# The first 400 steps of a hand-written schedule in another order: hourglass attention and a gated MLP on one core

## The chip, the core and the metric

The kernel runs on one NeuronCore of one Trainium2 chip. The metric is the device time of one execution in microseconds (us), as a median over several runs. A difference is given against the kernel before, which ran on the same chip. The profile is of one execution of its own, recorded by the hardware profiler, and its times are counted from the start of its span.

## What is computed

The inputs are q, k and v with 8 batches, 8 heads, 576 positions and 64 columns per head, and three weight matrices. Attention is computed twice, once on sequences averaged four to one and once on a band of seven positions, and both results are added. The sum, seen as 4608 tokens of 512 columns, goes through a gated MLP.

```python
q_d = q.reshape(B, H, Sd, 4, D).mean(axis=3)        # k_d, v_d likewise, Sd = 144
out_up = np.repeat(sm_attn(q_d, k_d, v_d), 4, axis=2)
mask = np.abs(pos[:, None] - pos[None, :]) < 4
scores = np.where(mask, scale * q @ k.T, -1e9)      # per head
out_local = softmax(scores) @ v
x = (out_up + out_local).transpose(0, 2, 1, 3).reshape(4608, 512)
out = (np.maximum(x @ w_gate, 0) * (x @ w_val)) @ w_out     # 512 -> 1536 -> 512
```

## The kernel before, in words

The work is cut two ways. Attention goes by pairs of heads: 8 batches of 4 pairs make 32 pairs, counted 0 to 31 (the first batch taken is batch 1). The MLP goes by chunks of 512 tokens, of which there are 9. Four pairs finish one batch of 576 tokens, so chunk 0 can start when pairs 0 to 3 are through attention, and from there on the attention of later pairs runs in between the matmuls of the MLP. The stage until both parts run side by side is the fill.

No scheduler decides the order. `SEQ` (L18 to L233) is one long string of 2097 words, and the last loop of the kernel takes them one after another; `emit_front` (its table is `FRONT_STEPS`) turns each into one or a few instructions. Every engine runs its own instructions strictly in the order of the list, and semaphores make an instruction wait for what it needs. A place in the list is thus a place in the queue of the engine that the step belongs to, and a step that waits holds up all that stands behind it on that engine, and nothing on the others but what depends on it.

The words that matter here, with pair `p`, part `i` and PSUM bank as numbers behind them:

- `loadq/p`, `loadk/p` (L454), `loadv/p` (L504): DMAs issued by GpSimd (POOL), which turn fp32 into fp16 on the way into the tiles `qk16_*` and `vw_*`. `wg/i`, `wv/i` (L1076) and `wo/i` (L1082) are quarters of the weights, 384 KB each, on the same queue. Pair 0's q alone is loaded by SyncE (SP) as fp32 into `q32`, and ScalarE (ACT) turns it into fp16 (`cast`, L1498). From pair 9 on, q and k come in halves (`qk/b0/0@0` and so on, L459).
- `ones/r` (L1504): GpSimd fills the second half of the blocks of `vw_4`, `vw_5` or `vw_6` with ones. `edge/i` (L791) are small fills by VectorE (DVE).
- `tr/p/i` (L540 for pairs 0 to 5, L556 for 6 to 8): TensorE (PE) transposes q and k into PSUM, 24 matmuls for a pair; `ev/p/..` (L576, L579) copies the result to SBUF by ACT or DVE. Later pairs are transposed by a DMA (`flip/p`, L520, on SP).
- `s1/p` (L637, L648): the scores; `ex/p`, `ed/p` (L658, L672): exponentials by ACT; `ma/p` (L664): the band's mask by DVE.
- `vd/p` (L618): six matmuls that pool v; `vc/p` (L627) copies them to SBUF.
- `su/p`, `sd/p` (L697, L685): weighted sums of pairs 0 to 3; `ru`, `tu`, `rd`, `td` (L709 to L728): their division; `xp/p` (L902, L904) and `xe/p` (L914): transposing into `xT`. From pair 4 on the steps are `den` (L738, L747), `num` (L759, L768), `ln`, `inv`, `xn` and `xsum`.
- `hg/j/k`, `hv/j/k` (L919): matmuls of chunk 0 with the gate and the value weights, each group of four followed by `relu` (L928, ACT) and `gate` (L931, DVE). `p/1` to `p/7` (L1004) multiply by the output weights, with sums and differences of blocks made by DVE (`wt`, `sum`, `next`).
- `warm/n` (L1089) and `brief/n` (L1099): n matmuls on zeros whose results nobody reads. Twelve wide ones (128x512) stand ahead of the list.
- `const` (L794): SP overwrites the zeros with a table for later pairs. It must wait for the last `warm`. `v4/a/0@1` (L511) is on SP too: two loads of v for pair 12.

GpSimd's DMAs use eight semaphores in turn, so each one waits until the one eight places ahead of it has landed; from the ninth on the queue is paced by landings.

Of the kernel before, what the change touches and what calls it, by code (L numbers as in the profile page):

```python
# [23 lines left out]
loadk/3 ev/2/01A/0 xp/0/0/4 ev/2/11A/2 ev/2/00A/0 xe/0/1V/5 s1/2/0 vc/1/6 sd/1/6 ma/1/1 rd/1/6 xe/0/0A/4 td/1/6 wv/0
wg/0 warm/3/7 su/1/4 loadk/4 ex/2/1/0 vd/2/6 ed/2/0 ex/2/0/0 tr/3/1/2 tr/3/2/3 vc/2/6 edge/1 wg/1 ru/1/4 tr/3/0/0
tu/1/0/4 tu/1/1/4 ev/3/21V/3 ev/3/11A/2 ev/3/10A/2 ev/3/01A/0 ev/3/00A/0 sd/2/6 xp/1/0/4 ev/3/20V/3 loadq/5 ma/2/0
xe/1/0A/4 xp/1/1/5 rd/2/6 s1/3/0 ma/2/1 loadk/5 ex/3/0/0 xe/1/1V/5 loadk/6 hv/0/0/7 loadv/4 su/2/4 td/2/6 ed/3/0
loadv/5 vd/3/6 ru/2/4 warm/4/1 tu/2/1/4 hv/1/0/1 ex/3/1/0 tu/2/0/4 tr/4/0/0 xp/2/0/4 ma/3/1 vc/3/6 ev/4/00A/0 loadq/6
xe/2/0A/4 wv/1 loadk/7 ma/3/0 xp/2/1/5 xe/2/1V/5 hv/1/1/1 loadq/7 sd/3/6 hv/0/1/7 su/3/4 rd/3/6 td/3/6 loadv/6
tr/4/1/2 hv/0/2/7 tr/4/2/3 hg/0/0/6 hg/0/1/6 ru/3/4 tu/3/0/4 ev/4/11A/2 ev/4/01A/0 ev/4/10A/2 tu/3/1/4 ev/4/20V/3  # L30
ev/4/21V/3 xp/3/1/5 xe/3/1V/5 xp/3/0/4 wg/2 xe/3/0A/4 hg/0/2/6 hg/1/0/0 s1/4/2 wv/2 wv/3 ex/4/0/2 ed/4/2 loadk/8
hg/1/1/0 hg/0/3/6 ma/4/0 wo/1 ex/4/1/2 hg/1/2/0 ma/4/1 wg/3 relu/0/6 hv/0/3/7 hg/1/3/0 relu/1/0 hv/1/2/1 tr/5/0/2
tr/5/2/4 loadv/7 tr/5/1/3 ev/5/11A/3 ev/5/00A/2 loadq/8 vd/4/6 vc/4/6 ev/5/21V/4 wo/0 ev/5/01A/2 ev/5/20V/4 hv/1/3/1
hg/3/*/0 wo/2 wo/3 ev/5/10A/3 hg/2/*/6 den/4/1/5 gate/0/7 gate/1/1 den/4/0/4 relu/3/0 qk/b3/0@0 tr/6/1/0 relu/2/6
loadv/8 hv/2/*/7 vd/5/1 num/4/1/3 qk/a2/1@0 ln/4 gate/2/7 ev/6/10A/0 inv qk/b0/0@0 num/4/0/2 s1/5/4 vc/5/1 hv/3/*/1
xn/2 ex/5/0/4 hg/4/*/2 ed/5/4 ev/6/11V/0 xsum/4 qk/a0/1@0 gate/3/1 tr/7/1/0 tr/6/0/4 tr/6/2/1 qk/b2/0@0 ex/5/1/4
ma/5/1 ev/6/20V/1 hv/4/*/3 ev/7/10V/0 hg/5/*/6 ev/7/11V/0 ev/6/21V/1 relu/4/2 ev/6/00A/4 vd/6/1 ev/6/01V/4 den/5/1/5
ma/5/0 qk/b1/0@0 flip/9 vc/6/1 gate/4/3 den/5/0/4 ln/4 num/5/0/2 num/5/1/3 relu/5/6 hv/5/*/7 inv hg/7/*/1 qk/a1/1@0
gate/5/7 relu/7/1 v/a/1@0 s1/6/4 ed/6/4 xn/2 v/b/0@0 ex/6/1/4 hv/8/*/0 v4/b/1@0 ex/6/0/4 ma/6/1 qk/a3/1@0 qk/b0/1@0
hv/7/*/3 sum/2/0@1 hg/8/*/2 relu/8/2 hg/6/*/7 tr/7/2/1 ma/6/0 tr/7/0/6 relu/6/7 gate/7/3 den/6/0/4 ev/7/00A/6 gate/8/0  # L40
ev/7/21A/1 edge/0 ev/7/20A/1 den/6/1/5 num/6/1/3 v4/a/0@1 qk/b1/0@2 tr/8/2/0 ln/4 xsum/5 ev/7/01V/6 num/6/0/2 v2/b/0@1
qk/b3/1@0 qk/b2/1@0 ev/8/21A/0 inv hv/6/*/7 gate/6/7 hv/9/*/1 ev/8/20A/0 s1/7/4 ed/7/4 ex/7/1/4 qk/b1/0@1 ex/7/0/4
hg/9/*/0 relu/9/0 xn/2 hg/10/*/3 qk/a1/0@1 hg/11/*/7 flip/10 hv/10/*/6 zs/0.1/0@1 ma/7/1 vd/7/4 ma/7/0 hv/11/*/0
relu/10/3 den/7/1/5 gate/9/1 xsum/6 vc/7/4 tr/8/0/1 relu/11/7 p/1/0@1 wt/0 keep/1/0@1 gate/10/6 gate/11/0 ev/8/01A/1
num/7/0/6 den/7/0/4 next/0/1@0 qk/a3/0@1 ln/4 num/7/1/7 tr/8/1/0 sumhi/0/0@1 qk/b1/1@0 p/2/0@1 qk/b0/0@1 next/1/1@0
ev/8/00A/1 wt/1 p/5/0@1 inv ev/8/10A/0 sumhi/1/0@1 wt/2 ev/8/11A/0 xn/6 p/6/0@1 xsum/7 flip/11 v/b/1@0 keep/2/0@1
vd/8/5 wt/3 zs/0.0/0@1 vc/8/5 qk/b2/0@1 p/7/0@1 scores/a/0@1 hg/0/0@1 exp/a0/0@1 keep/3/0@1 ed/a/0@1 qk/a2/0@1
mask/a0/0@1 hv/0/0@1 p/4/0@1 qk/b3/0@1 qk/a0/0@1 exp/a1/0@1 o/a10/0@1 mask/a1/0@1 v2/a/1@1 relu/0/0@1 o/a00/0@1
# [1531 lines left out]
```

## Time and profile before

| | |
|---|---|
| runs, us | 336.67, 337.72, 336.05; median 336.67 |
| profiled execution, us | 339.31 |
| span of its instructions, us | 337.5 |
| mean granted TensorE clock | 0.990 of full speed |

The profiled execution took 1.8 us longer than its span, and 2.6 us longer than the median of the runs. In the lines shown below, a row of a timeline begins with the start and the duration, both in us, then the engine, the line of the kernel, the operation, what it writes and reads, and how many in a row; in brackets stands how long the engine was idle before it and what ended that. Rows that are merged ("x24") give the time from the first start to the last end. In a table by windows each engine has its busy time in the window and its number of instructions; then come the granted clock, the share of the DMA engines (packets overlap, so it goes over 1) and GB/s. A DMA row ends in the KB moved by each DMA and the time from issue to landing.

### The profile page before, as it was taken

The page shows a single profiled execution, that of the slowest core. Times are in us where ns is not written, and L with a number is a line of the kernel's source. Part 1 is how long each engine was busy: PE and PEld are TensorE (multiplying, and loading weights), DVE is VectorE, ACT ScalarE, POOL GpSimd, SP SyncE. Part 2 cuts the span into 40 slices and gives each one's busy share as a digit, 9 for nine tenths or more (in the row PEclk, how much of TensorE's full clock was granted, in tenths as well). Part 3 has the DMA queues.
Part 4 walks back from the last instruction along what each step waited for, and adds up shares of the span by engine and source line. Part 5 has one row for each costly group of instructions (what it writes and reads, how often), then busy time and mean ns, then how long its engine had stood idle before and what let it go on. Part 6 is the DMA issues. An engine that isn't in the chain of part 4 may idle for free.

```text
span 337.5 us, 10448 instructions
## 1 busy us (share of the span) xinstructions
PE 328.8 (97%) x4176; PEld 237.9 (70%) x4176; DVE 284.4 (84%) x551; ACT 223.9 (66%) x553; POOL 182.4 (54%) x252
## 2 busy tenths in 40 slices
...
PEclk9959999999999999999999999999999999999999
...
GB/s 125 158 195 168 194 193 158 164 138 221 141 192 140 178 149 188 149 173 114 117 223 181 154 180 110 157 171 138 117 38 2 3 96 47 2 47 18 50 94 124
DMA packets 154966, 43.94 MB, mean 130 GB/s; under 512 B 139725, under 2 KB 149621, under 8 KB 154917
## 3 DMA queue, kind: packets, MB, share of 16 engines
...
q8 instruction: 32, 0.52, 0.7%
q14 instruction: 18, 0.14, 0.2%
q10 hardware_dynamic: 112, 0.04, 0.1%
...
## 4 chain that ended last, share of the span: by engine, by line
PE 87%; DVE 5%; POOL 3%; DMA 2%; issue 1%; ACT 1%; DVEq 0%; POOLq 0%
PE ps L919 28%; PE ps L1264 25%; PE ps L1167 18%; PE ps L852 6%; PE ps L1004 3%; DMA vw<-in_v_dram 2%; POOL qk L454 2%; DVE gT L1359 1%; PE ps L540 1%; PE ps L618 1%; DVE xT L1250 1%; DVE xo L998 1%; POOL vw L504 1%; PE ps L738 1%; PE ps L648 1%
## 5 line engine op out<-in xcount | busy, mean ns | idle before, releaser
L919 PE MATMUL ps<-xT,wv_sb 128*128 128x512 f16 x352 | 89.9, 380 | 0.0
L919 PEld LDWEIGHTS <-wv_sb 128*128 128x128 f16 x352 | 33.6, 98 | 27.4
L1275 ACT COPY ps<-ps 128x256 f32<-128x256 f32 x80 | 28.5, 365 | 19.6 <-PE ps L1264 16.5
L1264 PE MATMUL ps<-xT,qk 128*128 128x256 f16 x240 | 40.2, 273 | 0.2 <-DVE xT L1250 0.2
L1359 DVE SCALAR_TENSOR_TENSOR gT<-r,ps 128x512 f16<-128x512 f16 x55 | 37.2, 680 | 3.6 <-PE ps L919 2.6
L589 POOL TENSOR_TENSOR v<-v 112x384 f32<-112x384 f32 (+1 forms) x21 | 22.7, 1079 | 22.5 <-DMA v<-in_v_dram 22.0
L1264 PE MATMUL ps<-xT,wg_sb 128*128 128x256 f16 x180 | 31.4, 273 | 0.3 <-DVE r L1282 0.3
L1280 ACT CAST r<-ps 128x256 f16<-128x256 f32 x55 | 20.5, 376 | 16.6 <-PE ps L1264 12.0
L527 DVE TENSOR_REDUCE qkd<-qkT 128x288 f16<-128x1152 f16 x23 | 30.8, 1341 | 0.0
L1264 PEld LDWEIGHTS <-qk 128*128 128x128 f16 x240 | 22.7, 98 | 10.0 <-DVE xT L1250 0.4
L477 POOL DMA_DIRECT2D vw<-in_v_dram x40 | 29.0, 736 | 0.4 <-issue 0.2
L597 POOL TENSOR_TENSOR vd<-v 48x192 f16<-48x192 f32 x40 | 25.7, 642 | 5.8 <-PE ps L852 3.7
L919 PE MATMUL ps<-xT,wg_sb 128*128 128x512 f16 x104 | 26.3, 380 | 0.0
L1264 PEld LDWEIGHTS <-xo 128*128 128x128 f16 x240 | 23.1, 98 | 4.3 <-DVE xo L998 0.4
L1178 ACT COPY ps<-ps 128x256 f32<-128x256 f32 x54 | 19.2, 367 | 8.4 <-PE ps L1167 6.0
L459 POOL DMA_DIRECT2D qk<-in_q_dram x28 | 20.6, 736 | 7.7 <-PE ps L768 3.9
L1264 PE MATMUL ps<-wt,xo 128*128 128x256 f16 x180 | 23.9, 273 | 0.1
L459 POOL DMA_DIRECT2D qk<-in_k_dram x28 | 20.6, 739 | 2.7 <-DMA wg_sb<-in_moe_w_gate_dram 1.0
L1264 PEld LDWEIGHTS <-wg_sb 128*128 128x128 f16 x180 | 17.4, 98 | 6.7 <-issue 0.3
L931 DVE TENSOR_TENSOR gT<-r,ps 128x512 f16<-128x512 f16 x24 | 16.1, 679 | 5.9 <-PE ps L919 5.6
L1282 DVE TENSOR_TENSOR r<-ps,xT 128x256 f16<-128x256 f32 x44 | 17.5, 417 | 3.6 <-PE ps L1264 2.4
L1264 PEld LDWEIGHTS <-gT 128*128 128x128 f16 x180 | 17.4, 98 | 3.7 <-DVE gT L1359 0.9
...
## 6 DMA issues: line engine op xcount, KB each, us to landing
...
v<-in_v_dram SPq DMA_DIRECT2D x19, 192.0 KB, 5.9
...
v<-in_v_dram SPq DMA_DIRECT2D x21, 144.0 KB, 5.6
...
```

The lines of the kernel that those rows point to most:

```text
L459: nc.gpsimd.dma_start(dst.rearrange("p (j h d) -> p j h d", h=2, d=64)[:, :, hh, :], _dap(src, off + (1 - hh if hp >= NEW else hh) * S * D ...
L477: nc.gpsimd.dma_start(t[lo : lo + 64, j0:j1], _dap(v, base + j0 * QB * D, [[D, 64], [QB * D, j1 - j0], [1, D]]),)
L527: nc.vector.tensor_reduce(out=qkd[hp % 2].rearrange("p i t -> p (i t)"), in_=qkT[hp % 4][:, 0 : 2 * S].rearrange("p (t f) -> p t f", f=4), ...
L589: nc.gpsimd.tensor_tensor(out=m, in0=t[:, :, 0:128], in1=t[:, :, 128:256], op=ALU.add)
L597: nc.gpsimd.tensor_tensor(out=vp[hp % 3][lo : lo + 48, :, lo : lo + 64], in0=m[:, :, 0:64], in1=m[:, :, 64:128], op=ALU.add)
L852: nc.tensor.matmul(out=out, lhsT=left, rhs=right, start=zone not in begun, stop=True, skip_group_check=True)
L919: nc.tensor.matmul(out=out, lhsT=w[:, kk, bass.ts(jj, 128)], rhs=xT[:, kk, c * TCH : (c + 1) * TCH], start=(kk == 0), stop=(kk == 3),)
L1167: nc.tensor.matmul(out=out, lhsT=self.left[i][t], rhs=self.right[i][t], start=(i == 1 and t == 0), stop=(t == n - 1), skip_group_check=True,)
L1264: nc.tensor.matmul(out=out, lhsT=self.left[i - 1][k], rhs=self.right[i - 1][k], start=(i == 1 and k == 0), stop=(k == n - 1), skip_group_c ...
L1275: nc.scalar.copy(out=o, in_=x)
L1280: nc.scalar.copy(out=o, in_=self.d if i == 11 else self.a)
L1359: lambda c, jj, b, t: nc.vector.scalar_tensor_tensor(out=gT[c % 2][:, jj, :], in0=tg[t], scalar=0.0, in1=ps[:, b, :], op0=ALU.max, op1=ALU ...
```

## The change

Steps 2 to 418 of the list (about the first 400) stand in another order; they are the same steps with the same PSUM banks, and every later step keeps its place. Two lines of the diff show its form; the whole is 32 such lines against 32.

```diff
-cast ones/6 ones/4 ones/5 loadk/0 tr/0/0/2 ev/0/01A/2 pads ev/0/00A/2 tr/0/1/3 tr/0/2/4 ev/0/21V/4 ev/0/10A/3 loadq/1
+cast tr/0/0/2 ev/0/00A/2 loadk/0 loadv/0 pads tr/0/1/3 ev/0/10A/3 ev/0/11A/3 tr/0/2/4 vd/0/6 ev/0/01A/2 loadq/1
```

On GpSimd's queue, at the start of the program, the rows of the kernel before are these; `qk16_p` and `vw_p` are the tiles of pair p, and two more fills (`vw_6`, `vw_4`) stand ahead of the first row.

```order
L1504 MEMSET vw_5_87 112x12x64
L454 DMA qk16_0_72<-in_k_dram 96x6x128
L454 DMA qk16_1_73<-in_q_dram 96x6x128
L454 DMA qk16_1_73<-in_k_dram 96x6x128
L504 DMA vw_0_82<-in_v_dram 112x12x64
L454 DMA qk16_2_74<-in_q_dram 96x6x128
L454 DMA qk16_2_74<-in_k_dram 96x6x128
L504 DMA vw_1_83<-in_v_dram 112x12x64
L454 DMA qk16_3_75<-in_q_dram 96x6x128
L504 DMA vw_3_85<-in_v_dram 112x12x64
L454 DMA qk16_4_76<-in_q_dram 96x6x128
L504 DMA vw_2_84<-in_v_dram 112x12x64
```

The same queue now begins at once with loads:

```order
L454 DMA qk16_0_72<-in_k_dram 96x6x128
L504 DMA vw_0_82<-in_v_dram 112x12x64
L454 DMA qk16_1_73<-in_q_dram 96x6x128
L454 DMA qk16_1_73<-in_k_dram 96x6x128
L454 DMA qk16_3_75<-in_k_dram 96x6x128
L504 DMA vw_1_83<-in_v_dram 112x12x64
L454 DMA qk16_2_74<-in_q_dram 96x6x128
L454 DMA qk16_2_74<-in_k_dram 96x6x128
L504 DMA vw_2_84<-in_v_dram 112x12x64
L504 DMA vw_3_85<-in_v_dram 112x12x64
```

The load of v of pair 2 moved from the 11th to the 9th place among the loads, and the three fills of ones moved far back: the one of `vw_6` behind the 31st load, the other two further. The first value quarter (`wv/0`) is the 13th load in both; the first gate quarter moved from the 14th to the 15th place.

On TensorE, where the pooling matmuls of pair 2 (`vd/2`, on `vw_2`) begin, they stood right behind `su/1`:

```order
L697 LDWEIGHTS att_95
L697 MATMUL ps_113<-vw_1_83,att_95 128x65
L618 LDWEIGHTS cst_sb_68
L618 MATMUL ps_113<-vw_2_84,cst_sb_68 128x128
L618 LDWEIGHTS cst_sb_68
L618 MATMUL ps_113<-vw_2_84,cst_sb_68 128x128
```

Now six matmuls on zeros stand between, of which the last two are shown:

```order
L1089 LDWEIGHTS zero_sb_67
L1089 MATMUL ps_113<-zero_sb_67 128x248
L1089 LDWEIGHTS zero_sb_67
L1089 MATMUL ps_113<-zero_sb_67 128x248
L618 LDWEIGHTS cst_sb_68
L618 MATMUL ps_113<-vw_2_84,cst_sb_68 128x128
L618 LDWEIGHTS cst_sb_68
L618 MATMUL ps_113<-vw_2_84,cst_sb_68 128x128
```

These six (`warm/5` and `warm/1`) stood further ahead before; the same 20 narrow matmuls on zeros are in the list as a whole.

On SyncE's queue, behind the loads of the start, the transposing DMAs of pairs 9 to 11 and the loads for pair 12 stood like this:

```order
L1546 DMA cst_sb_68<-cst 72x288
L520 DMA_TRANSPOSE qkT_1_90<-qk16_2_74 128x12x96
L511 DMA v4_79<-in_v_dram 48x768
L511 DMA v4_79<-in_v_dram 64x768
L520 DMA_TRANSPOSE qkT_2_91<-qk16_3_75 128x12x96
L520 DMA_TRANSPOSE qkT_3_92<-qk16_4_76 128x12x96
L954 DMA out_0_dram<-y_sb_1118 128x512
L511 DMA v4_79<-in_v_dram 48x768
L511 DMA v4_79<-in_v_dram 64x768
L794 DMA zero_sb_67<-stk 128x640
```

Now the table and the two loads stand ahead of all transposes:

```order
L1546 DMA cst_sb_68<-cst 72x288
L794 DMA zero_sb_67<-stk 128x640
L511 DMA v4_79<-in_v_dram 48x768
L511 DMA v4_79<-in_v_dram 64x768
L520 DMA_TRANSPOSE qkT_1_90<-qk16_2_74 128x12x96
L520 DMA_TRANSPOSE qkT_2_91<-qk16_3_75 128x12x96
L520 DMA_TRANSPOSE qkT_3_92<-qk16_4_76 128x12x96
L954 DMA out_0_dram<-y_sb_1101 128x512
```

The table waits for nothing but the fill of the zeros and the last matmul on them, and the two loads behind it wait for nothing else.

More of the change, by code (lines that the diff above doesn't have):

```diff
@@ L24 @@
[L24 to L48, printed above, removed]
@@ L49 @@
-sum/3/0@1 c22//0@1 c11//0@1 o/a01/0@1 c21//0@1 qk/a1/1@1 o/a11/0@1 hg/1/0@1 hg/2/0@1 ln/a/0@1 next/0/0@1 inv/a/0@1
-v4/b/0@1 relu/1/0@1 const p/3/0@1 hg/3/0@1 relu/2/0@1 xn/a/0@1 v1/a/1@1 gate/0/0@1 c12//0@1 hv/2/0@1 xsum/a/0@1 vd/9/7
+cast tr/0/0/2 ev/0/00A/2 loadk/0 loadv/0 pads tr/0/1/3 ev/0/10A/3 ev/0/11A/3 tr/0/2/4 vd/0/6 ev/0/01A/2 loadq/1
+loadk/1 loadk/3 ev/0/21V/4 loadv/1 tr/1/0/7 ev/0/20V/4 s1/0/2 loadq/2 loadk/2 vc/0/6 ev/1/00A/7 tr/1/2/1 tr/1/1/0
+ev/1/01A/7 loadv/2 loadv/3 ed/0/2 warm/5/6 sd/0/6 loadq/3 loadk/4 wv/0 loadq/4 ex/0/0/2 brief/16/2 ev/1/21V/1
@@ new lines @@
+vc/2/6 xp/1/0/4 sd/2/6 ev/3/10A/2 xe/1/0A/4 rd/2/6 td/2/6 s1/3/0 su/2/4 vd/3/6 ex/3/0/0 wg/1 loadv/5 ru/2/4 tu/2/1/4
+tu/2/0/4 wv/1 hv/0/0/7 hv/0/1/7 ed/3/0 ex/3/1/0 tr/4/0/0 warm/4/1 ev/4/01A/0 wg/2 vc/3/6 xp/2/0/4 ev/4/00A/0 xe/2/0A/4
+xp/2/1/5 ma/3/0 hv/1/0/1 loadq/6 loadk/8 loadk/7 loadv/6 ma/3/1 loadq/7 sd/3/6 hv/1/1/1 wv/2 xe/2/1V/5 su/3/4 rd/3/6
+tr/4/2/3 tr/4/1/2 td/3/6 ev/4/11A/2 ev/4/10A/2 loadv/7 ru/3/4 tu/3/0/4 tu/3/1/4 hg/0/0/6 hg/0/1/6 hv/0/2/7 hg/1/0/0
+wv/3 ones/6 ev/4/21V/3 loadq/8 ev/4/20V/3 wg/3 xp/3/1/5 xp/3/0/4 hv/1/2/1 hg/0/2/6 wo/1 xe/3/1V/5 wo/0 wo/2 xe/3/0A/4
@@ new lines @@
+s1/4/2 ex/4/0/2 hg/0/3/6 relu/0/6 hv/1/3/1 hv/0/3/7 hg/1/1/0 hg/1/2/0 hg/1/3/0 vd/4/6 ed/4/2 tr/5/0/2 tr/5/1/3
+ex/4/1/2 tr/5/2/4 ev/5/01A/2 relu/1/0 vc/4/6 ev/5/10A/3 ev/5/11A/3 ev/5/00A/2 gate/0/7 ma/4/0 ma/4/1 hv/2/*/7 hg/2/*/6
+relu/2/6 ev/5/20V/4 ev/5/21V/4 gate/1/1 den/4/1/5 den/4/0/4 ln/4 inv gate/2/7 num/4/1/3 num/4/0/2 xn/2 vd/5/1 hg/3/*/0
+vc/5/1 s1/5/4 ex/5/0/4 hv/3/*/1 ex/5/1/4 ed/5/4 hg/4/*/2 hg/5/*/6 relu/3/0 relu/4/2 hv/4/*/3 ma/5/0 ma/5/1 tr/6/0/4
+gate/3/1 xsum/4 gate/4/3 relu/5/6 tr/6/1/0 ev/6/00A/4 ev/6/11V/0 ev/6/01V/4 ones/4 num/5/0/2 den/5/1/5 tr/6/2/1
@@ new lines @@
+ev/6/10A/0 wo/3 num/5/1/3 qk/b1/0@0 den/5/0/4 const v4/a/0@1 ln/4 ev/6/21V/1 ev/6/20V/1 hv/5/*/7 gate/5/7 inv vd/6/1
+tr/7/1/0 xn/2 vc/6/1 loadv/8 ev/7/10V/0 s1/6/4 hg/7/*/1 qk/b3/0@0 ed/6/4 qk/b2/0@0 qk/a1/0@1 qk/b0/0@0 hg/8/*/2
+v/b/0@0 ev/7/11V/0 qk/a0/1@0 ex/6/1/4 hv/8/*/0 v/a/1@0 hg/6/*/7 relu/8/2 ma/6/1 qk/a3/1@0 relu/7/1 qk/a2/1@0 ex/6/0/4
+hv/7/*/3 gate/8/0 ma/6/0 qk/a1/1@0 num/6/0/2 tr/7/2/1 relu/6/7 den/6/1/5 gate/7/3 tr/8/2/0 ev/7/20A/1 qk/b2/0@1
+ev/7/21A/1 ev/8/21A/0 ev/8/20A/0 flip/9 xsum/5 den/6/0/4 num/6/1/3 sum/2/0@1 tr/7/0/6 ev/7/00A/6 hv/6/*/7 ev/7/01V/6
@@ new lines @@
+flip/10 gate/6/7 ln/4 inv qk/b2/1@0 hv/9/*/1 xn/2 qk/a0/0@1 s1/7/4 hg/9/*/0 ex/7/0/4 vd/7/4 ex/7/1/4 relu/9/0 xsum/6
+v4/b/1@0 wt/0 hg/10/*/3 ma/7/1 ma/7/0 hv/11/*/0 ed/7/4 relu/10/3 gate/9/1 hg/11/*/7 ones/5 hv/10/*/6 qk/b1/1@0 vc/7/4
+qk/b0/1@0 p/1/0@1 relu/11/7 gate/11/0 den/7/1/5 keep/1/0@1 den/7/0/4 gate/10/6 ln/4 tr/8/0/1 sumhi/0/0@1 next/0/1@0
+ev/8/00A/1 num/7/1/7 num/7/0/6 sumhi/1/0@1 wt/1 tr/8/1/0 inv qk/a2/0@1 p/2/0@1 ev/8/11A/0 ev/8/01A/1 vd/8/5 p/5/0@1
+qk/b3/1@0 ev/8/10A/0 next/1/1@0 xn/6 vc/8/5 xsum/7 p/6/0@1 scores/a/0@1 exp/a1/0@1 qk/b3/0@1 wt/2 zs/0.1/0@1 hv/0/0@1
```

13 lines of the change are left out of this document (9 added, 4 removed).

## Prediction

> **What bounds the kernel now.** I read the page first, then TensorE's waits, its windows over the first 28 us, the timeline of the places where it waits, and the DMA issues.
>
> ```profile
> PE 328.8 (97%) x4176; PEld 237.9 (70%) x4176; DVE 284.4 (84%) x551; ACT 223.9 (66%) x553; POOL 182.4 (54%) x252
> PEclk9959999999999999999999999999999999999999
> PE 87%; DVE 5%; POOL 3%; DMA 2%; issue 1%; ACT 1%; DVEq 0%; POOLq 0%
> ```
>
> TensorE is 97% busy and makes up 87% of the chain that ends last, so its queue sets the time. The one place where its clock is not full is the third slice of 8.4 us, inside the part that the change reorders. POOL's and DMA's 5% of the chain lie there too.
>
> ```profile
> PE ps L618 <- DMA vw<-in_v_dram: 1.5, 1, 1.5
> PE ps L1089 <- DVE zero_sb L407: 1.3, 1, 1.3
> PE ps L540 <- DMA qk<-in_q_dram: 1.2, 1, 1.2
> ```
>
> Apart from the start, TensorE waits twice: 1.2 us for pair 1's q, and 1.5 us for pair 2's v. Waits after that are 0.3 us or less, so whatever TensorE gains early can be carried to the end, as long as what it needs comes earlier too.
>
> ```profile
> 0.00:2.00 2.00, 0.74 (x2) 0.28 (x3) 1.01 (x4) 1.26 (x1) 1.47 (x6) 1.00 0.07 15
> 2.00:4.00 2.00, 2.00 (x6) 0.76 (x5) 1.67 (x4) 0.02 (x1) 2.00 (x4) 1.00 0.90 251
> 6.00:8.00 2.00, 0.81 (x20) 0.46 (x16) 0.72 (x2) 1.15 (x4) 2.00 (x4) 1.00 1.55 140
> 16.00:18.00 2.00, 0.79 (x19) 0.64 (x15) 1.70 (x6) 1.51 (x3) 1.36 (x2) 1.00 1.68 185
> 18.00:20.00 2.00, 1.71 (x24) 1.52 (x26) 0.18 (x1) 0.70 (x3) 1.58 (x3) 0.61 1.35 210
> 20.00:22.00 2.00, 2.00 (x26) 1.50 (x22) 1.55 (x5) 1.25 (x4) 0.67 (x2) 0.50 1.46 187
> 22.00:24.00 2.00, 2.00 (x32) 1.56 (x31) 0.78 (x2) 1.41 (x4) 1.40 (x2) 0.50 1.41 197
> 24.00:26.00 2.00, 2.00 (x22) 1.45 (x19) 1.70 (x5) 0.73 (x2) 0.83 (x2) 0.68 1.95 173
> 26.00:28.00 2.00, 2.00 (x42) 1.58 (x38) 1.42 (x5) 0.78 (x2) 1.73 (x2) 1.00 2.40 157
> ```
>
> Right behind the wait at 16 to 18 us the granted clock falls to half until about 25 us. The timeline shows what that costs: the same 24 matmuls of a pair's transposes take 0.94 us before and 1.65 us in it.
>
> ```profile
> 0.74 2.08 POOL vw L1504 x3
> 10.76 7.49 DMA vw<-in_v_dram
> 4.18 0.83 ACT L1498 CAST qk<-q 96x768 f16<-96x768 f32 x1 [2.17 <-DMA q<-in_q_dram]
> 5.68 1.21 PE L540 MATMUL ps<-gT,qk 96*64 96x144 f16 x24
> 13.25 0.94 PE L540 MATMUL ps<-gT,qk 96*64 96x144 f16 x24
> 16.26 0.53 PE L697 MATMUL ps<-vw,att 112*128 112x65 f16 x12
> 18.29 0.71 PE L618 MATMUL ps<-vw,cst_sb 112*128 112x128 f16 x6 [1.50 <-DMA vw<-in_v_dram]
> 18.93 1.65 PE L540 MATMUL ps<-gT,qk 96*64 96x144 f16 x24
> ```
>
> The first two rows are from the chain of waits: GpSimd fills ones for 2.08 us before it issues its first load, and the load of pair 2's v, issued at 10.76, lands 7.49 us later, at 18.25.
>
> **The change part by part.** The sum is made at the first gate matmul (`hg/0/0`, at 28.76), by when both orders have done nearly the same work, and then followed through chunk 0.
>
> *The wait for pair 2's v* (gain 1.5). Its load moves from the 11th place to the 9th and the fills of 2.08 us ahead of it go. The first nine loads are now six of 144 KB and three of 168 KB, as they were; so v of pair 2 lands where the ninth landed (about 2 us before 18.25), less what the earlier start gives. TensorE reaches `vd/2` after the six zero matmuls put ahead of it, no earlier than at 16. The load has about 1 us of slack; if that is gone, the wait returns one for one.
>
> *The half clock* (gain 3.3). Busy time times the missing clock is 1.71 x 0.39 + 2.00 x 0.50 + 2.00 x 0.50 + 2.00 x 0.32 = 3.3 us. It comes back if the wait is what lets the clock fall. The Trainium skill ("TensorE: Matmul & The Clock Gate", section "Part 1: The HAM clock gate") says that the clock goes to half after at least one idle window of about 3.4 us; here a wait of 1.5 us stands ahead of the drop, so the trace does not agree with it as it is worded, and by that rule this term would be nil.
>
> *The wait for pair 1's q* (gain 0.2, from -0.8 to 1.2). That load is now third on the queue instead of second but starts earlier. Against it, GpSimd's first loads now fall into 2 to 4 us, when SP's loads alone move 251 GB/s, and pair 0's q, on which the cast at 4.18 and all else hangs, gets slower. The cast has 0.67 us of slack (it ends at 5.01, the first transpose starts at 5.68 behind the wide zero matmuls). I take most of the gain as eaten.
>
> *New waits up to 28 us* (cost 0.6, from 0 to 1.5). Work on pairs 0 and 1 is no longer interleaved as it was; scores of pair 2 now follow `sd/1` and must wait for copies that ACT makes. Walking through both queues with the durations of these rows I find some 0.2 us at each of three places.
>
> *Loads that are late for a TensorE that is ahead* (cost 0.9, from 0 to 2.0).
>
> ```profile
> wv_sb<-in_moe_w_val_dram POOLq DMA_DIRECT2D x1, 384.0 KB, 8.6
> wg_sb<-in_moe_w_gate_dram POOLq DMA_DIRECT2D x1, 384.0 KB, 9.7
> 12.40 0.86 POOL L1076 DMA_DIRECT2D wv_sb<-in_moe_w_val_dram  x1
> 13.17 0.83 POOL L1076 DMA_DIRECT2D wg_sb<-in_moe_w_gate_dram  x1
> 28.76 0.60 PE L919 MATMUL ps<-xT,wg_sb 128*128 128x512 f16 x2
> qk<-in_q_dram POOLq DMA_DIRECT2D x1, 144.0 KB, 9.9
> 16.57 0.74 POOL L454 DMA_DIRECT2D qk<-in_q_dram  x1 [1.07 <-DMA vw<-in_v_dram]
> 32.15 0.98 PE L540 MATMUL ps<-gT,qk 96*64 96x144 f16 x24
> zero_sb<-stk SPq DMA_DIRECT2D x1, 160.0 KB, 3.6
> v<-in_v_dram SPq DMA_DIRECT2D x1, 192.0 KB, 5.8
> v<-in_v_dram SPq DMA_DIRECT2D x1, 144.0 KB, 6.4
> ```
>
> The first weight quarters land at 12.40 + 8.6 = 21.0 and 13.17 + 9.7 = 22.9, so one takes 1.9 us of the queue. The gate quarter is used at 28.76 (5.9 us of slack), pair 5's q lands at 16.57 + 9.9 = 26.5 and is used at 32.15 (5.7 us). With TensorE 4 to 5 us ahead and the loads 1 to 2 us, 2 to 3 us of slack are left. But SP now issues the table and pair 12's v (160 + 192 + 144 = 496 KB) right behind the last zero matmul, at some 21 us, into the busiest part; at 251 GB/s that is 2.0 us if GpSimd's loads stand still meanwhile, and nothing if they share freely. I take 0.9 of waiting, near the middle.
>
> *Chunk 0* (cost 0.6, from 0 to 3.0).
>
> ```profile
> 30.00:40.00 10.00, 10.00 (x137) 5.79 (x135) 5.51 (x12) 9.09 (x20) 6.27 (x8) 1.00 1.67 190
> 40.00:50.00 10.00, 10.00 (x112) 5.23 (x110) 6.84 (x16) 6.28 (x12) 5.00 (x7) 1.00 1.62 189
> ```
>
> TensorE has no gap here now, so a new order can only lose. ACT is at 9.09 of 10, and pair 4's logarithm, inverse and pair 5's copy now follow each other on it while `hv/3` and `hg/5` wait for their banks; a couple of waits of 0.3 us are likely.
>
> *After the 400 steps* nothing is given back: the transposing DMA of pair 9 is issued at 59.08, lands 7.2 us later at 66.3, and DVE first reads it at 72.10, which leaves 5.8 us.
>
> ```profile
> 59.08 1.67 SPq L520 DMA_TRANSPOSE qkT<-qk  x1
> qkT<-qk SPq DMA_TRANSPOSE x1, 7.2
> 72.10 1.34 DVE L527 TENSOR_REDUCE qkd<-qkT 128x288 f16<-128x1152 f16 x1
> ```
>
> The fills of ones cost POOL the same 2.08 us later, between landings that it waits for anyway; the small fills of `edge` and the rest of the DVE steps change place only.
>
> Sum: 1.5 + 3.3 + 0.2 - 0.6 - 0.9 - 0.6 = 2.9 us. The profiled execution would go from 339.31 to 336.4; the median of the runs, 2.64 lower, from 336.67 to 333.8.
>
> **The rivals.**
>
> *The half clock is not the wait's to give.* It may belong to that one execution (which took 2.6 us longer than the median), or be due to something that stays. By the Trainium skill's rule on the idle window ("TensorE: Matmul & The Clock Gate", section "Part 1: The HAM clock gate") it would be so, and that section adds that the windows run free and the change-over varies from run to run. For it: 1.5 us is little idle time, and 6 to 8 us has as much (0.81 busy of 2.00) without a drop. Against: the drop starts at the very end of the wait. Then TensorE is only 1.7 us ahead, loads keep their slack, and 1.5 + 0.2 - 0.3 = 1.4 us are left: 335.3.
>
> *The drop moves.* If pair 0's q comes late, the idle time at 6 to 8 us (1.19 now) grows past the 1.5 us that preceded the drop, and the clock halves at 8 us instead. The sum loses its 3.3 and is -0.4: 337.1.
>
> *Slower: ACT sets chunk 0.* If ACT, at 9.09 of 10, is late in freeing banks in the new order, TensorE waits at the 24 groups of four matmuls of chunk 0. At 0.3 us each this is 7.2 instead of 0.6, and 2.9 becomes -3.7: 340.4. It decides from 0.15 us per group on (3.5 us instead of 0.6), where the gain is gone.
>
> *All goes well:* the sum without its two last costs is 4.4 us: 332.3, or 331.7 without the new waits either.
>
> **How the numbers follow.** The forecast of 333.8 gets 0.41, the half clock not removed 0.21, the moved drop 0.12, ACT 0.16, all well 0.10. I call 0.5%, 1.7 us, the least that a measurement of this kernel tells from no change, so faster means below 335.0 and slower above 338.4. Faster: 0.37 of the forecast, 0.03 and 0.02 of the next two, 0.10 of the last, 0.52. Slower: 0.14 of ACT, 0.03 of the first two rivals, 0.17. The rest, 0.31, is within. The range is 332.0 to 337.6: it takes in the forecast with its bounds (a gain of 1.0, with the loads at 2.0 and chunk 0 at 1.4, to 4.6, with the three costs together at 0.4 instead of 2.1), both clock rivals and most of the good case, and leaves out most of ACT's 0.16. The forecast's own range is 332.1 to 335.7.
>
> **What would show it.** Right: TensorE's wait for `vw` at L618 gone, no window under full clock in 16 to 28 us, `hg/0/0` at about 24 to 25 us, loads landing with little slack at 25 to 40 us, and waits of TensorE at L919 of no more than 1 us together. Wrong: a window at half clock anywhere else, a first transpose later than 6.4, or TensorE waiting repeatedly for ACT or for weight quarters between 28 and 60 us. If the clock is full and the first gate matmul early, but the end is not, the loss lies in chunk 0.

## The result and the profile after

The kernel after takes 335.18 us (median of 20 runs), the kernel before 337.13 in the same rounds; the ratio is 0.9941, 95% interval 0.9923 to 0.9959. Run again later it was 335.58 against 336.84, ratio 0.9967 (0.9946 to 0.9988). So 0.3 to 0.6% is gained, 1.3 to 2.0 us. Two of the 20 executions of after show a lower clock, one of 340.23 us at 0.995 and a disturbed one of 473.86 us at 0.658, and one of before is disturbed (666.18 us); the ratio leaves these three out (with the one of 340.23 it would be 0.995). The profiled execution of after took 335.85 us with a span of 334.1, against 339.31 and 337.5 before: some 3.4 us less, about twice what the runs show. Where the difference between these two numbers lies is the main lesson of this case.

Three lines of the page of after answer to those of before:

```profile
PE 327.0 (98%) x4176; PEld 235.6 (71%) x4176; DVE 287.1 (86%) x551; ACT 223.9 (67%) x553; POOL 183.2 (55%) x252
PEclk9999999999999999999999999999999999999999
PE 72%; DMA 10%; DVE 9%; POOL 4%; issue 2%; ACT 1%; DVEq 0%; ACTq 0%; POOLq 0%
```

The third slice of the clock is full now. TensorE is the chain for 72% instead of 87%, and DMA for 10% instead of 2%: with TensorE ahead, loads set part of the end. TensorE's waits:

```profile
PE ps L1089 <- DVE zero_sb L407: 1.3, 1, 1.3
PE ps L618 <- ACT qkd L579: 0.7, 1, 0.7
PE ps L540 <- DMA qk<-in_q_dram: 0.4, 1, 0.4
PE ps L919 <- ACT y_sb L1049: 0.2, 1, 0.2
```

The wait for pair 2's v (1.5 us) is gone, the one for pair 1's q went from 1.2 to 0.4, and one of 0.7 us is new. The windows of after, 2 us each, and two rows of TensorE's timeline:

```profile
6.00:8.00 2.00, 1.72 (x32) 1.13 (x30) 0.71 (x2) 1.21 (x5) 2.00 (x4) 1.00 1.83 167
16.00:18.00 2.00, 2.00 (x39) 1.72 (x37) 1.97 (x6) 1.71 (x6) 1.95 (x3) 1.00 1.46 195
18.00:20.00 2.00, 2.00 (x52) 1.84 (x50) 1.57 (x6) 1.80 (x5) 0.88 (x2) 1.00 1.42 208
```

```profile
16.21 0.50 PE L618 MATMUL ps<-vw,cst_sb 112*128 112x128 f16 x6
23.52 0.60 PE L919 MATMUL ps<-xT,wg_sb 128*128 128x512 f16 x2
```

`vd/2` (at 16.21) follows the zero matmuls without a wait, 16 to 20 us is all work at full clock, and the first gate matmul starts at 23.52 instead of 28.76. Where the new wait comes from is read from the chain of waits between 10 and 80 us:

```profile
12.44 9.58 DMA wg_sb<-in_moe_w_gate_dram
22.30 12.56 DMA wg_sb<-in_moe_w_gate_dram
38.97 12.17 DMA wo_sb<-in_moe_w_out_dram
51.23 0.96 DVE wt L970
55.41 0.15 ACT qkT L579
56.90 0.51 PE ps L618 x6
```

Each load row is the time from issue to landing. GpSimd's queue of loads has no lead left: a quarter of the output weights lands at 38.97 + 12.17 = 51.14, DVE starts on it at once (51.23), what stands behind that on DVE comes late, and TensorE waits for it at 56.9.

### The profile page after: what moved, and what is told of

It reads as the page before. It is cut to its first block, busy times and chain, and to the rows that moved or that the text cites. A ratio compares the mean times of both kernels' runs of the same rounds, so it can differ in the third digit from the quotient of the medians.

```text
span 334.1 us, 10441 instructions
## 1 busy us (share of the span) xinstructions
PE 327.0 (98%) x4176; PEld 235.6 (71%) x4176; DVE 287.1 (86%) x551; ACT 223.9 (67%) x553; POOL 183.2 (55%) x252
## 4 chain that ended last, share of the span: by engine, by line
PE 72%; DMA 10%; DVE 9%; POOL 4%; issue 2%; ACT 1%; DVEq 0%; ACTq 0%; POOLq 0%
PE ps L1264 23%; PE ps L919 20%; PE ps L1167 18%; PE ps L852 7%; DMA wg_sb<-in_moe_w_gate_dram 7%; DMA wo_sb<-in_moe_w_out_dram 4%; PE ps L1004 2%; POOL qk L454 2%; DVE xo L998 2%; DVE xT L1250 2%; POOL vw L504 1%; DVE gT L1359 1%; DVE xn L880 1%; DVE gT L931 1%; DVE xT L886 1%
## 5 line engine op out<-in xcount | busy, mean ns | idle before, releaser
L1264 PE MATMUL ps<-xT,qk 128*128 128x256 f16 x240 | 40.2, 273 | 0.2 <-DVE xT L1250 0.2
L1264 PE MATMUL ps<-xT,wg_sb 128*128 128x256 f16 x180 | 31.4, 273 | 0.2 <-DVE r L1282 0.2
L1264 PEld LDWEIGHTS <-qk 128*128 128x128 f16 x240 | 22.7, 98 | 10.4 <-issue 0.9
L1264 PEld LDWEIGHTS <-xo 128*128 128x128 f16 x240 | 22.9, 98 | 4.8 <-DVE xo L998 0.8
L1264 PE MATMUL ps<-wt,xo 128*128 128x256 f16 x180 | 23.8, 273 | 0.2 <-DVE xo L998 0.2
L1264 PEld LDWEIGHTS <-wg_sb 128*128 128x128 f16 x180 | 17.3, 98 | 6.7 <-issue 0.4
L1282 DVE TENSOR_TENSOR r<-ps,xT 128x256 f16<-128x256 f32 x44 | 17.6, 418 | 3.7 <-PE ps L1264 2.1
L1264 PEld LDWEIGHTS <-gT 128*128 128x128 f16 x180 | 17.4, 98 | 4.1 <-issue 1.2
```

The costliest lines, as they stand in the source:

```text
L1264: nc.tensor.matmul(out=out, lhsT=self.left[i - 1][k], rhs=self.right[i - 1][k], start=(i == 1 and k == 0), stop=(k == n - 1), skip_group_c ...
```

## The experiments

The first theory was the prediction's: pair 2's v comes late, TensorE waits, the wait lets the clock fall, and the change takes all three away. The rivals were that the half clock belongs to something else, that the gain comes from the order of the computation, and that SP's loads, now early, cost part of it.

**One part alone: the fills of ones.** Of the whole change only this (pieces of the list, with the neighbours):

```diff
-cast ones/6 ones/4 ones/5 loadk/0
+cast loadk/0
...
+loadv/6 ones/6
...
+ev/6/01V/4 ones/4
...
+hg/11/*/7 ones/5
```

> The kernel before with one part of the change: GpSimd's three fills of ones (2.08 us) go from ahead of its first load to the places that they have in the kernel after; all else is in the old order. Theory (the wait lets the clock fall): the load of pair 2's v lands some 1.5 to 2 us earlier, TensorE's wait for it at L618 shrinks from 1.50 us to 0.3 or less, and no window up to 28 us is under full clock, so that this one part brings most of the whole change: 1.5 to 2.5 us off the median, ratio about 0.994. Rival (the half clock is not the wait's): the wait goes, but windows between 15 and 28 us at half clock remain in the profile or in most runs, and the median falls by 1.5 us at most. Second rival (the order of the computation matters more than the loads): less than 0.5 us.

Measured: 335.55 us, ratio 0.9951 (0.9932 to 0.9969). In its profile these are what is left of TensorE's waits at the two places:

```profile
PE ps L618 <- DVE ru L722: 0.4, 1, 0.4
PE ps L540 <- DMA qk<-in_q_dram: 0.2, 1, 0.2
```

Neither load is waited for by more than 0.2 us. The mean clock of an execution tells whether it holds a drop to half clock: it is about 0.995 or 0.990 with one, and 0.998 or more without. Of 12 executions none is under 0.998. Three words of the list, moved, give what the reordering of 400 steps gives, within the uncertainty (335.55 against 335.18 and 335.58; by the ratios 0.9951 against 0.9941 and 0.9967).

**Zero matmuls in the wait.** The kernel before with `warm/5` and `warm/1` directly ahead of `vd/2`:

```diff
-tu/0/1/4 warm/5/7 rd/0/6
+tu/0/1/4 rd/0/6
...
-xp/0/1/5 warm/1/7 loadq/4
+xp/0/1/5 loadq/4
...
-ex/2/1/0 vd/2/6
+ex/2/1/0 warm/5/7 warm/1/7 vd/2/6
```

> The kernel before with two of its wide zero matmul steps (warm/5 and warm/1) moved directly ahead of the value product of pair 2 at which TensorE waits; loads and all else as before. The wait for v stays, TensorE is only busy in part of it (some 1.3 us of zero matmuls). Theory (idle time ahead of 18.4 us lets the clock fall): the clock stays full from 16 to 28 us, and the profiled span falls by about 3 us, the median by as much as the runs of before have the dip. Rival (the half clock is not the idle time's): 18 to 25 us still runs at about 0.5, and the time is within 0.5 us of before. Moving the two steps takes cover from their old places, which can cost up to 0.5 us either way.

Measured: 336.93 us, ratio 0.9991 (0.9968 to 1.0013), one of 12 executions with a clock of 0.995. It tells nothing apart, for the reason that the records of the clock in the same rounds gave: of 29 executions of before, only 4 have the drop at all. There was little to be cured.

**SP's loads late.** The kernel after, with two words about where they stood before:

```diff
-den/5/0/4 const v4/a/0@1 ln/4
+den/5/0/4 ln/4
...
+flip/9 v4/a/0@1
...
+relu/1/0@1 const
```

> The kernel after with two of SP's loads back at late places in the order (the table of 160 KB after the second scaling of the list's gate, pair 12's v of 192 KB after the transposing DMA of pair 9); all else as after. Theory (SP's early loads hold GpSimd's back): the second gate quarter lands at about 27.5 us instead of 29.6, the later quarters about 2 us earlier, DVE's wait for wo at L970 (1.4 us) is gone, and 1 to 2 us come off the time of after: about 333.5. Rival (the queues share, and what is late is GpSimd's own queue of loads): landings within 0.7 us of after, time within 0.5 us of it. Third: the table or pair 12's v is now late where it is used, and the time is up to 2 us longer.

Measured: 334.95 us, ratio 0.9930 (0.9903 to 0.9957). First the kernel after: POOL's issue of the second gate quarter, SP's issues, and the time from issue to landing of loads issued from 17 to 24 us.

```profile
17.63 0.78 POOL L1076 DMA_DIRECT2D wg_sb<-in_moe_w_gate_dram  x1
21.44 0.34 SPq L794 DMA_DIRECT2D zero_sb<-stk  x1
21.82 1.03 SPq L511 DMA_DIRECT2D v<-in_v_dram  x2
```

```profile
wg_sb<-in_moe_w_gate_dram POOLq DMA_DIRECT2D x1, 384.0 KB, 12.0
zero_sb<-stk SPq DMA_DIRECT2D x1, 160.0 KB, 7.2
```

And with SP's loads late:

```profile
17.66 0.77 POOL L1076 DMA_DIRECT2D wg_sb<-in_moe_w_gate_dram  x1
```

```profile
wg_sb<-in_moe_w_gate_dram POOLq DMA_DIRECT2D x1, 384.0 KB, 9.3
```

Issued at the same time, the quarter lands at 27.0 instead of 29.6, and the issues behind it on GpSimd's queue are earlier by 2.2 to 2.9 us. So 496 KB from SP delay a queue of loads by some 2.7 us. The Trainium skill ("DMA: Bandwidth & Descriptors", section "Queues, rings and completion order") says that each DMA engine goes round between the queues that have work for it; the 12.0 us against 9.3 agree with that, but do not show it by themselves. DVE's wait for the output weights and the new wait of TensorE are gone, and at 94 us this execution is 0.9 us ahead of that of after (table below). In the profile the lead is lost again at 185 us, in a wait of 1.2 us for a load of the list; in the median 0.2 to 0.6 us are left (0.4 to 1.2 by the ratios), which the runs cannot tell from nothing.

**The new loads under the old computation.** The first 24 loads in the new order at the head of the list (the fills of ones late), the rest as before:

```diff
-cast ones/6 ones/4 ones/5 loadk/0 tr/0/0/2
+cast loadk/0 loadv/0 loadq/1 loadk/1 loadk/3 loadv/1 loadq/2 loadk/2 loadv/2
...
```

> The kernel before with the new order of GpSimd's first loads (and the fills of ones late), the computing steps in the old order. Theory (the gain is in the loads, not in the order of the computation): TensorE's waits for q of pair 1 (1.2 us) and v of pair 2 (1.5 us) are both 0.3 or less, the clock is full, and the median is at or below that of after, 335 us or some tenths less, since SP's table stays late as well. Rival (the computing order is needed to use the loads): another load is now last, TensorE waits 1 us or more for a k or q of pair 2 or 3, and the gain is under 1 us.

Measured: 337.47 us, ratio 0.9992 (0.9973 to 1.0011), a drop of the clock in 2 of 12 executions. The rival was right, though the load that is last now belongs to another pair than it named:

```profile
PE ps L556 <- DMA qk<-in_q_dram: 1.5, 1, 1.5
PE ps L540 <- DMA qk<-in_q_dram: 0.8, 1, 0.8
```

Now q is late, once for a pair that is transposed at L556 (pairs 6 to 8). The gain of the early start, 1.8 us in the run with the ones late (337.34 to 335.55), is spent.

**Before once more**, for a profile at full clock.

> The kernel before once more, for a profile without the half clock: of 29 timed executions of it 25 show a granted clock of 0.998 or more (median 337.1 us) and 4 one of 0.990 to 0.995 (338.2 to 338.7 us). Theory (the dip belongs to some executions only): a clock of 1.000 in this one, span near 335.4 us, the wait for pair 2's v still 1 us or more, and from the first gate matmul on some 3 us ahead of the first profile of before. Against the kernel after, the lead that is left is 1 to 2 us. Rival: a clock near 0.990 again, so that the 29 records don't tell it.

Measured: 337.01 us (8 runs), ratio 0.9998 (0.9971 to 1.0025); profiled execution 337.45 us, span 335.7, clock 1.000. Two of its waits, two windows, and its first gate matmul:

```profile
PE ps L618 <- DMA vw<-in_v_dram: 1.1, 1, 1.1
PE ps L540 <- DMA qk<-in_q_dram: 1.0, 1, 1.0
```

```profile
16.00:18.00 2.00, 0.90 (x21) 0.75 (x18) 1.73 (x6) 1.48 (x3) 1.47 (x2) 1.00 1.58 193
6.00:28.00 22.00, 19.66 (x383) 15.21 (x383) 14.99 (x43) 15.62 (x41) 17.28 (x23) 1.00 1.83 171
```

```profile
25.83 0.60 PE L919 MATMUL ps<-xT,wg_sb 128*128 128x512 f16 x2
```

The wait is there (0.90 busy of 2.00 from 16 to 18 us), the drop is not, and the first gate matmul starts at 25.83, 2.9 us earlier than in the first profile of the same kernel. Of these 2.9 us, 0.4 is the shorter wait for v (1.1 instead of 1.5). This profile is the fair base. Against it, the starts of three matmuls of TensorE, read from the timelines (the last is the first matmul of the final stage):

| profiled execution | first gate matmul | first at L1264 | first at L1167 |
|---|---|---|---|
| before, clock full (base) | 25.83 | 94.17 | 261.52 |
| before, first profile | +2.9 | +2.9 | +1.9 |
| after | -2.3 | -1.3 | -1.6 |
| after, once more | -2.2 | -1.6 | -0.3 |
| ones late | -1.5 | -1.1 | -1.8 |
| after, SP's loads late | -2.2 | -2.2 | -1.4 |
| ones twice | +2.1 | +3.0 | +1.8 |
| after, ones first | +0.4 | +0.9 | +0.3 |
| after, old loads | +2.9 | +2.9 | +1.0 |
| after, ones first, wait filled | +1.5 | +1.6 | -0.5 |
| after, fewer zeros | -2.7 | -2.6 | -3.5 |
| after, no zeros | -3.0 | -2.3 | -2.5 |

Up to 94 us the two executions of after, at the same clock, agree within 0.3 us; from there to the final stage the difference to the base moves by up to 1.3 us one way and 2.0 the other, about as much as the runs of one kernel differ. The first column flatters the rows that begin with after: in their order `hv/0/2`, one matmul of 0.38 us, stands behind the first gate matmul, in the order of before ahead of it, so 0.4 us of their lead there is work not yet done.

**The fills twice.** The suspected cost doubled:

```diff
-cast ones/6 ones/4 ones/5 loadk/0
+cast ones/6 ones/4 ones/5 ones/6 ones/4 ones/5 loadk/0
```

> The kernel before with the three fills of ones done twice, so that GpSimd's first load starts another 2.08 us late; the fills repeat the same values. Theory (what the change gains is the start of the loads): the waits for pair 1's q and pair 2's v grow by about 2 us in all, the median by 1.5 to 2.1 us, to about 339, since loads behind them are late by the same. For the clock: if a longer wait lets it fall more often, 0.990 to 0.995 shows in most of the runs rather than in 4 of 29. Rival (later slack takes it up): under 0.7 us.

Measured: 339.34 us, ratio 1.0062 (1.0039 to 1.0086), 2.2 us over before, about the 2.08 us that the loads start later; the waits are now 2.2 us for a k and 1.1 us for a q. The clock: 0.989 to 0.995 in all 12 executions, against 3 of the 31 of before in the same rounds. With the start that much later the drop came every time; how much of the 2.2 us is the drop is not told apart.

**After, with the ones first:**

```diff
-cast tr/0/0/2 ev/0/00A/2
+cast ones/6 ones/4 ones/5 tr/0/0/2 ev/0/00A/2
...
```

The three words are gone from their late places.

> The kernel after with the three fills of ones (2.08 us) ahead of GpSimd's first load again, as before; all else as after. Theory (the start of the loads is the gain): 1.5 to 2.1 us slower than after, so about 337 us, no gain over before. Rival (the new order has slack for it): less than 0.7 us slower than after.

Measured: 338.19 us, ratio 1.0036 (1.0011 to 1.0062), so 2.6 to 3.0 us slower than after, more than expected, and slower than before. In the new order v of pair 0 is wanted first, and TensorE waits 1.4 us for it, until 8.8 us. The clock is under 0.998 in 11 of 12 executions. In the profile:

```profile
8.00:10.00 2.00, 1.17 (x22) 0.89 (x23) 0.09 (x1) 0.58 (x3) 2.00 (x3) 0.91 1.71 162
10.00:12.00 2.00, 2.00 (x34) 1.60 (x29) 0.71 (x2) 1.75 (x5) 2.00 (x4) 0.50 1.99 155
12.00:14.00 2.00, 2.00 (x39) 1.72 (x38) 0.64 (x4) 0.94 (x3) 2.00 (x4) 0.74 2.08 161
```

A mean of 0.91 over 2 us is half clock for 0.09 x 2 / 0.5 = 0.36 us, so it falls at 9.64; 0.74 gives 1.04 us, up to 13.04. That is 3.4 us; one drop of this length makes the mean clock of the whole execution 0.995. The same sum on the first profile of before (0.61 from 18 to 20 us, 0.68 from 24 to 26) gives 18.44 to 25.28, 6.84 us or two times 3.42 (mean clock 0.990). In these traces the clock is set in steps of 3.41 us, and the step ahead of each drop can be laid out as a window of its own, below.

**The new order of the computation over the old loads**, with the ones first:

```diff
-cast tr/0/0/2 ev/0/00A/2 loadk/0 loadv/0 pads
+cast ones/6 ones/4 ones/5 loadk/0 loadq/1 loadk/1 loadv/0 loadq/2 loadk/2 loadv/1
...
```

> The kernel after with GpSimd's first loads in the old order and the fills of ones first; the computing steps, and SP's loads, as after. It is the new order of the computation alone. Theory (the orders of loads and computation belong together): TensorE waits for a v or k of pairs 1 and 2, the time is above that of before, 338 to 341 us. Rival (the order of the computation gains by itself): below before by 0.7 us or more, 336.4 or less.

Measured: 339.92 us, ratio 1.0077 (1.0051 to 1.0104), clock 0.988 to 0.990 in all 8 executions. The first theory was right on the time; the load that is waited for is v of pair 0:

```profile
PE ps L618 <- DMA vw<-in_v_dram: 3.1, 1, 3.1
```

So the order of the loads and the order of the computation only work together: each alone, measured against the same start of the loads, costs 1.9 us (337.47 against 335.55) or 2.8 us (339.92 against 337.17). The 2.8 us hold more than the order: the clock drops in all 8 executions, and SP's loads are early, as in after.

**Zero matmuls in the wait, where the drop is common.** The kernel with the ones first, in the new order, and 13 extra zero matmuls:

```diff
-tr/0/2/4 vd/0/6
+tr/0/2/4 warm/13/6 vd/0/6
```

> The kernel of the run with the ones first in the new order, with 13 extra zero matmuls (some 1.35 us) directly ahead of the value product of pair 0 at which TensorE waited 1.4 us; the load and the end of the wait stay where they were. In that run the window of 3.41 us that held the wait was idle for 1.50 us, the clock halved behind it, and 11 of 12 executions show 0.989 to 0.995. Theory (the idle time in a window, and not the late load, lets the clock fall): a clock of 0.998 or more in at least 10 of 12 executions, and 336.4 to 337.2 us instead of 338.2. Rival (the drop is due to something else that the late start brings): the clock falls as often as before, and the time is 338 us or more.

Measured: 338.17 us, ratio 1.0031 (1.0003 to 1.0059), clock under 0.998 in 2 of 12 executions (0.995 and 0.997) instead of 11. The drop is rare now though the load is issued as late as before. On the time the theory fails: 338.17 against 338.19 us, no gain, though the two intervals leave room for one of 1 us. The profiled execution, one of the two with a drop, shows where the wait goes:

```profile
6.81 1.55 PE L1089 MATMUL ps<-zero_sb 128*128 128x248 f16 x13
8.39 0.49 PE L618 MATMUL ps<-vw,cst_sb 112*128 112x128 f16 x6
10.35 0.44 PE L540 MATMUL ps<-gT,qk 96*64 96x144 f16 x8 [1.46 <-DMA qk<-in_q_dram]
```

And the run with the ones first, without the filling:

```profile
8.77 0.50 PE L618 MATMUL ps<-vw,cst_sb 112*128 112x128 f16 x6 [1.44 <-DMA vw<-in_v_dram]
9.32 0.44 PE L540 MATMUL ps<-gT,qk 96*64 96x144 f16 x8
```

Pair 0's v is now used at 8.39, without a wait, but pair 1's q, ready by 9.32 in the run without the filling, holds TensorE up until 10.35, for 1.46 us. In this execution the idle time has only moved to the next load, and the first gate matmul is about 1 us later than without the filling. Why the q lands later, and whether the ten executions at full clock wait there too, is not shown. If they do, a wait of the same length let the clock fall in 11 of 12 executions and in 2 of 12, and its length alone does not decide.

With the five profiles that have a drop, the last step of 3.41 us ahead of it can be read. In order: before, the ones twice, after with the ones first, after over the old loads, and the wait filled (the second number is TensorE's busy time).

```profile
15.03:18.44 3.41, 1.92 (x46) 1.61 (x45) 2.84 (x9) 2.37 (x6) 1.93 (x3) 1.00 1.84 181
```

```profile
7.82:11.23 3.41, 1.83 (x48) 1.48 (x50) 0.72 (x2) 1.40 (x5) 3.41 (x6) 1.00 1.69 139
```

```profile
6.23:9.64 3.41, 1.91 (x39) 1.44 (x38) 0.72 (x2) 1.49 (x5) 3.41 (x5) 1.00 1.70 146
```

```profile
5.95:9.37 3.42, 1.25 (x26) 0.86 (x25) 0.72 (x2) 1.15 (x4) 3.42 (x6) 1.00 1.68 134
```

```profile
8.01:11.43 3.42, 1.93 (x40) 1.39 (x39) 0.00 (x0) 0.97 (x4) 3.42 (x5) 1.00 1.93 164
```

And the idlest steps that were followed by no drop, in the first and in the second profile of before:

```profile
4.79:8.20 3.41, 2.17 (x34) 1.14 (x33) 1.70 (x10) 1.37 (x5) 3.41 (x5) 1.00 1.47 135
```

```profile
15.82:19.24 3.42, 2.23 (x51) 1.80 (x49) 2.02 (x7) 2.20 (x6) 2.60 (x4) 1.00 1.51 195
```

With 1.93 us of work or less in 3.41 (57%) the clock fell, with 2.17 or more (64%) it did not, and in the nine profiles without a drop no step between the first transposes and 28 us has less than 2.2. One step speaks against a line between them: 4.40 to 7.82 in the run with the ones twice, 1.66 us busy, no drop; most of that work is wide zero matmuls. Where the steps begin differs from one execution to the next (15.03 in one profile of before, 15.82 in the other), so a wait of 1 to 1.5 us can fall into one step or into two. That this decides how often the clock falls is argued, not shown. It also stays open why a drop lasts one step in some profiles and two in others: TensorE was busy all through the first step of half clock both in before (two steps) and with the ones first (one). Over all timed runs with a record of the clock, before shows the drop in 11 of 109 executions: 338.46 us against 336.96 without it (medians).

**Without the zero matmuls.** With the loads early they may be mere work. First the run with SP's loads late without those from `vd/2` on (13, not the 15 that the expectation counts):

```diff
-td/1/6 warm/5/7 warm/1/7 vd/2/6
+td/1/6 vd/2/6
...
-ev/3/21V/3 warm/3/7 xp/1/1/5
+ev/3/21V/3 xp/1/1/5
...
-tr/4/0/0 warm/4/1 ev/4/01A/0
+tr/4/0/0 ev/4/01A/0
```

> The kernel of the run with SP's two loads late, without four of its steps of zero matmuls (15 matmuls, those ahead of pair 2's value product and the two steps behind it; in after's profile they take some 1.9 us of TensorE). They compute nothing that is used; they kept TensorE busy where it would wait. Theory (with the loads early and the clock full they are only work): 0.8 to 1.9 us less than the run with SP's loads late, about 333.6. Rival 1 (other waits stand in their place): within 0.5 us of it. Rival 2 (the idle time that comes instead lets the clock fall): 0.995 in a good part of the executions and 336 us or more.

> The kernel after once more, on the same chip and in the same rounds as the two others, as their base. All theories: 334.8 to 335.6 us, a clock of 0.998 or more in all undisturbed executions.

Measured: 334.81 us, ratio 0.9937 (0.9911 to 0.9963), and for after in the same rounds 335.58, ratio 0.9967, with the clock full in all 12 as expected. By the median it is rival 1: no difference from the run with SP's loads late (ratio 0.9930). At the first gate matmul its profile is 0.4 us ahead of that run (23.17 against 23.58), so of 1.9 us of zero matmuls most was cover. Without them the clock is full in all 12 executions too.

Then without the last three such steps:

```diff
-ed/0/2 warm/5/6 sd/0/6
+ed/0/2 sd/0/6
...
-ex/0/0/2 brief/16/2 ev/1/21V/1
+ex/0/0/2 ev/1/21V/1
...
-ma/0/1 warm/2/7 ex/1/0/0
+ma/0/1 ex/1/0/0
```

> The kernel of the run with fewer zero matmuls, without the last three such steps too (7 of 248 columns and 16 narrow ones between 9.5 and 11.8 us, some 1.6 us of TensorE), so that from the first transposes on TensorE runs no zero matmuls. They stand where the next matmul needs what DVE and ACT make of pair 0's scores. Theory A (they only fill time that TensorE would wait): the idle time of 1.2 to 1.6 us appears in their place, the first gate matmul starts within 0.4 us of the run before, and, as this idle time can fall into one window of 3.41 us with the wait for pair 1's q, the clock falls in some of the executions (0.995 in 1 to 6 of 12); the median is 334.5 to 335.6 us, no gain. Theory B (they are work): idle time under 0.8 us, clock full in all, 0.8 to 1.4 us less, about 333.7.

Measured: 333.59 us, ratio 0.9898 (0.9878 to 0.9918), the fastest version here, faster than after as well (335.18 and 335.58; the interval lies below both of its intervals). The clock is full in all 6. Waits take the place of the larger part of the zeros:

```profile
10.53 0.25 PE L637 MATMUL ps<-qkd 64*72 64x144 f16 x2 [0.62 <-ACT qkd L576]
11.58 0.48 PE L697 MATMUL ps<-vw,att 112*128 112x65 f16 x10 [0.28 <-DVE att L664]
```

```profile
9.83:13.24 3.41, 2.52 (x61) 2.05 (x58) 2.96 (x9) 3.41 (x10) 3.41 (x6) 1.00 2.13 164
```

The idlest step has 2.52 us of work, above what let the clock fall elsewhere; it idles 0.9 us, between what the two theories say. The first gate matmul is 0.3 us earlier than in the run before it, as theory A has it, while the clock and the median are those of theory B. The medians differ by 1.2 us; this much the traces do not show, the two were measured on different chips, and their intervals overlap, so only the 0.3 us are accounted for.

## Why the prediction was right or wrong

The forecast of 333.8 was 1.4 us under the 335.18 measured, and the sign and the range held, but the largest term of the sum did not. Going through it:

**The wait for pair 2's v** (1.5): right. It is gone, and what it is worth at full clock is 1.1 us. What removed it is the early start of the queue more than the new place: the run with only the ones late has no wait for it either.

**The half clock** (3.3): this is the step that failed. That idle time lets the clock fall is borne out: the steps ahead of the five drops have 1.25 to 1.93 us of work, no step of the profiles without one has less than 2.2 (the one step of 1.66 us stays against it), and the drop came in all 12 executions with the ones twice. But the sum was made on one execution and carried over to the median: "The profiled execution would go from 339.31 to 336.4; the median of the runs, 2.64 lower". Most of these 2.64 us were the drop itself: with 0.4 us of longer wait it put that execution 2.9 us behind the base at the first gate matmul, so some 2.5 us are the drop's, and 1.9 us were left of the 2.9 at the start of the final stage. The drop is in 11 of 109 executions and costs 1.5 us between the medians, so its share in an average run is about 0.15 us, not 3.3. The mean clock of 0.990 and the 2.6 us above the median, both known, said so together. The Trainium skill ("TensorE: Matmul & The Clock Gate", section "Part 1: The HAM clock gate") says that the windows run free and that the change-over varies between runs; the two profiles of before agree with that. Its condition of an idle window of about 3.4 us does not hold as it is worded: 1.91 to 1.93 us of work in 3.41 did not keep the clock up in three of the profiles.

**The wait for pair 1's q** (0.2, up to 1.2): 0.6, from 1.0 in the second profile of before to 0.4. The early start was worth more than the third place cost: with the ones late and the old place 0.2 is left.

**New waits up to 28 us** (cost 0.6): not there. From 6 to 28 us, of after:

```profile
6.00:28.00 22.00, 21.56 (x406) 16.55 (x406) 16.04 (x44) 17.21 (x44) 17.30 (x22) 1.00 1.79 188
```

TensorE idles 22.00 - 21.56 = 0.44 us, of which the wait for q is 0.4, against 22.00 - 19.66 = 2.34 in the fair base. These 1.9 us are most of the 2.3 by which the first gate matmul is earlier; the other 0.4 is no gain but `hv/0/2`, by which the two orders had not done the same work there.

**Loads that are late for a TensorE that is ahead** (cost 0.9): near in size, in part by luck. SP's 496 KB delay GpSimd's queue by 2.7 us, more than the 2.0 that the prediction took as the most, and at 94 us the run without them is 0.6 to 0.9 us further ahead than the two executions of after. The wait is not for the loads whose slack the prediction counted (the gate quarter and pair 5's q) but for a quarter of the output weights.

**Chunk 0** (cost 0.6, up to 3.0): no cost shows. From the first gate matmul to 94 us, after falls back from -2.3 to -1.3, and the run with SP's loads late stays at -2.2. As 0.4 us of either lead at the first gate matmul is `hv/0/2`, the new order without SP's loads gains some 0.3 us here. ACT never sets TensorE back by more than 0.2 us there, but for the wait that the late weights cause.

**After the 400 steps** (nothing): right on the whole (-1.3 becomes -1.6 in one execution, and -1.6 becomes -0.3 in the other). The 5.8 us of slack of pair 9's transposing DMA, however, were nearly used up: issued at 58.77, it lands 7.3 us later, at 66.1, and is read at 67.14. Of the 23 reductions that read these DMAs, DVE waits for one in this profile, the next, by the page of after (the last two columns):

```profile
L527 DVE TENSOR_REDUCE qkd<-qkT 128x288 f16<-128x1152 f16 x23 | 30.8, 1342 | 0.4 <-DMA qkT<-qk 0.4
```

With the half clock left out, the profiled executions give 337.45 - 335.85 = 1.6 us, inside what the runs show (1.3 and 2.0). The terms as measured add up to 1.1 + 0.6 + 0.2 + 0.3 - 0.9 = 1.3 us at 94 us (the 0.2 is what is left of the 1.9 us of idle time); with the 0.15 of the half clock it is 1.5 instead of 2.9. That the forecast was no further off is luck: the half clock was some 3.1 us too large, and more than half of that was made up by waits and costs of the new order that did not come.

**The rivals.** "The half clock is not the wait's to give" gave 335.3, which is nearly what was measured, and for its first reason: the drop belonged to that execution and some 10% of the others. For its other reason, that something else lets the clock fall, no run speaks. "The drop moves" did not happen in the two profiles of after (the one execution at 0.995 has no profile); it is what happens when the new order gets the old start (from 9.6 us on in the run with the ones first). "ACT sets chunk 0" did not happen.
